# A fused attention and two-layer MoE kernel: batch 0's x transposed in full blocks, batch 1's scores moved into the first softmax, state reads held back

## The chip, the core and the metric

The kernel runs on one core of a Trainium2 chip. The core has TensorE (PE, matmuls and transposes, results into PSUM), ScalarE (ACT, activations and copies), VectorE (DVE, elementwise work and reductions), GpSimd (POOL) and SyncE (SP); SP and POOL issue the loads here. The metric is device time of one execution in microseconds (us), lower is better.

## The reference

```python
# x: (4, 8, 512, 64)   state: (4, 8, 32, 64)
scores = scale * x @ state.T                 # softmax over the 32 state rows
xread  = softmax(scores) @ state             # 512 rows
scores2 = scale * state @ x.T                # softmax over the 512 rows of x
sread  = softmax(scores2) @ x                # 32 rows
attn = concatenate([xread, sread], axis=2)   # (4, 8, 544, 64)
h = tokens(attn) @ w_in                      # 2176 tokens x 512, w_in 512 x 2048
y = (h - tanh(h)) @ w_out                    # w_out 2048 x 512
h2 = y @ w2_in
out = (h2 * tanh(softplus(h2))) @ w2_out
```

The weights are given as float64 and reach the kernel as pairs of 32-bit words. Everything is wanted to float32 precision.

## The kernel before

**Work and order.** The tokens run in the order batch 0, 1, 2, the state rows of all batches ("s"), batch 3; after that the second layer follows in five blocks. A batch of the first layer has 16 steps `t`, one for each 128 columns of `w_in`. A step computes `h` with six matmuls of 512 columns (`up_x`), applies the nonlinearity (`elem1`: one `t` and one `gh` activation on ACT, `t` and `gl` on DVE) and three steps later adds the product with `w_out` into four accumulators (`down_x`, twelve matmuls). Each fp32 product is made of three matmuls of high and low parts (`mm3p`); the first three steps of batch 0 use plain fp32 instead (`PLAIN`), eight longer matmuls a step.

**The fold.** xread is never formed. `sw(b, c)` multiplies the state by `w_in` (tile `swp` in PSUM, `swh` and `swl` in SBUF), once for every four steps, and `up_x` multiplies it by the transposed softmax `AT` (`ath`, `atl`). For batch 0 the first four pieces are made one by one (`sw_first`, `f0` to `f3`).

**Attention of a batch.** Load x (`load_x`, four tiles of 256 KB), transpose it (`xt_t`, PSUM tile `xtp`) and copy it to SBUF (`xt_c`, tile `xt`), scores (`sc_m`, PSUM `sct`), copy (`sc_c`, `scs`), transpose the scores (`sc_t`, `sc`), softmax on DVE and ACT (`sc_max`, `sc_sub`, `sc_exp`, `nm_sum`, `nm_rec`, `nm_mul`: tiles `mx`, `a`, `sm`), transpose the result (`at_a_hi`, `atp`, `ath`). The state read uses the same scores the other way round: `at_exp_t` (softmax along the rows, on `scs`), `at_read_t` (transposes, `e2p`), `at_sread` (matmuls `srd`). State itself is transposed by `state_t` (`stt`, `sbp`, `sbt`).

**Weights.** Each of the 64 weight tiles is a load of 512 KB into one of three buffers (`stage`, tile `st`), and is turned into float32 by `conv_steps`: two activations (`w`, `r`) and a combination on DVE. After the second activation the buffer is free, and the next load goes out on SP's queue. Tiles 1 to 4 are `w_in` of the first 512 columns; after them `w_in` and `w_out` tiles alternate.

**What sets the order.** A scheduler orders the instructions of each engine by the order in which the program emits them and by its own estimates; every engine then works in that fixed order and waits where an operand is missing. The start is written out by hand in `FIRST_STEPS`: up to the bar, PE, ACT and DVE each keep exactly the order of the list (class `Pinned`). The letters: `k` warm-up matmuls on a tile of zeros, `s` state, `x`/`X` transposes of batch 0's x and their copies, `w` the next third of a weight conversion, `c`/`C` scores and copies, `t` `m` `b` `e` `u` `v` `y` the softmax steps, `h`/`l` the halves of `AT`, `f` the pieces of `sw`. After the bar comes the loop over all steps, with side work hung on steps by `at(step, fn)`: for batch 1, loads at steps 1 to 4, transposes at 5 to 8, scores at 9, softmax at 11 to 13, and the state reads of batches 0 and 1 at 19 to 23. Since the scheduler may pull side work forward, parts of it run much earlier than their step. Loads of x go out on SP's queue for batches 0 and 1 and on POOL's for 2 and 3.

**Storage.** 97 SBUF slots of 256 KB are handed out in turn (`get`, `put`). PSUM has eight banks; in the start all but one serve as side banks (`side_bank`), afterwards two (`s0`, `s1`), for `swp`, `xtp`, `sct`, `sc`, `e2p` and `srd`.

Of the kernel before, what the change touches and what calls it, by code (L numbers as in the profile page):

```python
# [29 lines left out]

FIRST_LOADS = "s0123wwwt"
FIRST_STEPS = """
    k4 s0 x0 X0 x1 X1 x2 X2 x3 X3 w0 w0 w0 c0 C0 C1 k2 t0 m0 t1 w1 w1 b0 m1 f0 e0 b1 k12 w2
    u0 v0 y0 e1 w2 h0 u1 v1 y1 h1 l0 w1 l1 | f1 w2 f2 w3 w3 w3 f3
"""
BLOCKS = [4, 4, 4, 3, 2]

# [7 lines left out]
class Pinned:  # L45


    def __init__(self, engine, order):
        self.engine, self.order = engine, order
        self.on, self.last, self.floor = False, None, None  # L50

    def __getattr__(self, name):
        fn = getattr(self.engine, name)

        def call(*args, **kw):
            i = fn(*args, **kw)  # L56
            before = self.last if self.on else self.floor
            if before is not None:
                self.order(i.ins, before)
            if self.on:  # L60
                self.last = i.ins
            return i

        return call
# [3 lines left out]
def attention_moe_kernel(  # L68
# [17 lines left out]
    T = S + NS  # L86
    scale = 1.0 / float(D) ** 0.5

    def order(after, before):
        tc.add_manual_dep(  # L90
            after, before.name,
            mybir.DependencyInfo(mybir.DependencyClass.NoSync, mybir.DependencyReason.DATA),
            reason="activation table",
        )

    TE, AC, V = (Pinned(e, order) for e in (nc.tensor, nc.scalar, nc.vector))
# [13 lines left out]
    def put(*units):  # L110
        for u in units:
            free.append(u.slot)
# [9 lines left out]
    SB = get("sbt")  # L122
    XS = get("xst")
    xst = XS.t.rearrange("p (k n) -> p k n", k=KD)

    def head(b, k, i):
        c = (b * KD + k) * NS
# [109 lines left out]
    X, A, AT = {}, {}, {}  # L237
    XT, SC, ET = {}, {}, {}

    def load_x(b, ks=range(KD)):  # L240
        q = nc.gpsimd if b > 1 else nc.sync
        for k in ks:
            u = get("x", newest=b > 1)
            if b:
                q.dma_start(
                    out=u.t.rearrange("p (r h d) -> p r h d", r=4, h=2),
                    in_=x[b, 2 * k:2 * k + 2].rearrange("h (p r) d -> p r h d", r=4),
                )
            else:
                q.dma_start(  # L250
                    out=u.t.rearrange("p (h c) -> p h c", h=2),
                    in_=x[b, 2 * k:2 * k + 2].rearrange("h (p r) d -> p h (r d)", r=4),
                )
            X[b, k] = u

    def x_tile(b, k, i, r):
        c = r * 128 + i * 64 if b else i * 256 + r * 64
        return X[b, k].t[:, c:c + 64]
# [6 lines left out]
    def xt_t(b, k):  # L265
        P["x", b, k] = ps = side_bank("xtp")
        for r in range(4):
            if b:
                TE.transpose(
                    out=ps[:, r * 128:(r + 1) * 128],  # L270
                    in_=X[b, k].t[:, r * 128:(r + 1) * 128],
                    identity=ident,
                )
                continue
            for i in range(2):
                TE.matmul(
                    out=ps[i * 64:(i + 1) * 64, r * 128:(r + 1) * 128],
                    lhsT=x_tile(b, k, i, r),
                    rhs=ident,
                    start=True,  # L280
                    stop=True,
                )

    def xt_c(b, k):
        XT[b, k] = get("xt")
        AC.activation(out=XT[b, k].t, in_=P.pop(("x", b, k)), func=ACTF.Copy)

    def at_xt(b, k):
        xt_t(b, k)
        xt_c(b, k)  # L290

    def sc_m(b):
        P["c", b, 0], P["c", b, 1] = by_head("sct", b, [[XT[b, k].t for k in range(KD)]])
        put(*(XT.pop((b, k)) for k in range(KD)))

    def sc_c(b, j):
        SC[b, j] = get("scs")
        AC.activation(out=SC[b, j].t, in_=P.pop(("c", b, j)), func=ACTF.Copy)

    def at_scores(b):  # L300
        sc_m(b)
        for j in range(2):
            sc_c(b, j)
# [55 lines left out]
    def at_exp_t(b, j):  # L359
        e = SC.pop((b, j))  # L360
        mt = small.tile([128, 2], F32, tag="mt", name="mt")
        V.tensor_reduce(out=mt[:, 0:1], in_=e.t, axis=AX.X, op=ALU.max)
        V.tensor_scalar(
            out=mt[:, 0:1], in0=mt[:, 0:1], scalar1=-scale, scalar2=None, op0=ALU.mult
        )
        AC.activation(
            out=e.t, in_=e.t, func=ACTF.Exp, scale=scale, bias=mt[:, 0:1], accum_out=mt[:, 1:2]
        )
        V.tensor_scalar(
            out=mt[:, 1:2], in0=mt[:, 1:2], scalar1=1e-9, scalar2=None, op0=ALU.add  # L370
        )
        V.reciprocal(out=mt[:, 1:2], in_=mt[:, 1:2])
        V.tensor_scalar(
            out=e.t, in0=e.t, scalar1=mt[:, 1:2], scalar2=None, op0=ALU.mult
        )
        ET[b, j] = e

    def at_read_t(b, j):
        ps = side_bank("e2p")
        e = ET.pop((b, j))  # L380
        for r in range(4):
            TE.transpose(
                out=ps[:, r * 128:(r + 1) * 128],
                in_=e.t[:, r * 128:(r + 1) * 128],
                identity=ident,
            )
# [127 lines left out]
    def evac(dst, src, i):  # L514
        if i % 2:
            return V.tensor_copy(out=dst, in_=src)
        return AC.activation(out=dst, in_=src, func=ACTF.Copy)
# [216 lines left out]

    side = {}

    def at(step, fn):
        side.setdefault(step, []).append(fn)

    seq = []  # L740
    start = {}
# [16 lines left out]
    for b in (1, 2, 3):  # L758
        for c in range(4):
            at(start[b] + 4 * c - 2, lambda b=b, c=c: sw(b, c))  # L760
    for k in range(KD):
        at(1 + k, lambda k=k: load_x(1, (k,)))
        at(5 + k, lambda k=k: at_xt(1, k))
    at(9, lambda: at_scores(1))
    for j in range(2):
        at(11 + j, lambda j=j: at_exp(1, j))
        at(12 + j, lambda j=j: at_norm(1, j))
        for b in range(2):
            k = 19 + b + 2 * j
            at(k, lambda b=b, j=j: (at_exp_t(b, j), at_read_t(b, j)))  # L770
            if j:
                at(k + 1, lambda b=b: at_sread(b))
    for b in (2, 3):
        at(start[b - 1], lambda b=b: load_x(b))
        for i, f in enumerate(at_steps(b)):
# [28 lines left out]
    def state_t(g, u):  # L804
        ps = side_bank("sbp")
        for e in range(4):
            for i in range(2):
                TE.matmul(
                    out=ps[i * 64:(i + 1) * 64, e * 128:(e + 1) * 128],
                    lhsT=u.t[:, e * 64:(e + 1) * 64],  # L810
                    rhs=ident,
                    start=True,
                    stop=True,
                )
        for i in range(2):
            p = slice(i * 64, (i + 1) * 64)
            AC.activation(
                out=SB.t[p, g * 256:(g + 1) * 256].rearrange("p (e n) -> p e n", n=NS),
                in_=ps[p].rearrange("p (e i n) -> p e i n", i=2, n=NS)[:, :, i, :],
                func=ACTF.Copy,  # L820
            )
        put(u)

    nc.scalar.preload_act_table_set("exp_and_others")
# [22 lines left out]
    def conv_first(f):  # L847
# [3 lines left out]

    steps = {
        "x": lambda k: xt_t(0, k), "X": lambda k: xt_c(0, k), "s": lambda j: state_t(j, st[j]),
        "c": lambda j: sc_m(0), "C": lambda j: sc_c(0, j), "t": lambda j: sc_t(0, j),
        "m": lambda j: sc_max(0, j), "b": lambda j: sc_sub(0, j), "e": lambda j: sc_exp(0, j),
        "u": lambda j: nm_sum(0, j), "v": lambda j: nm_rec(0, j), "y": lambda j: nm_mul(0, j),
        "h": lambda j: at_a_hi(0, j), "l": lambda j: at_a_lo(0, j), "f": sw_first,
        "w": conv_first, "k": keep_warm,
    }
    for e in (TE, AC, V):  # L860
        e.on = True
    for key in FIRST_STEPS.split():
        if key == "|":
            for e in (TE, AC, V):
                e.floor, e.on = e.last, False
        else:
            steps[key[0]](int(key[1:]))
    put(warm)
# [33 lines left out]

    low = 0
    for i in range(len(seq) + 2):
        q = seq[i] if i < len(seq) else None
        prev = [seq[i - k][1:] if start["2"] <= i - k < len(seq) else None for k in range(3)]
        if q:
            up(q)
        if prev[0]:
            up_2(*prev[0], prev[2])  # L910
        elif prev[2]:
            elem2_hi(*prev[2])
        if prev[1]:
# [12 lines left out]
        late_conv(i)  # L926
        AC.on, V.on = pinned
# [33 lines left out]
```

## Time and profile before

| | us |
|---|---|
| median of three runs | 752.68 (751.9 to 754.49) |
| the profiled execution | 752.56 |
| its span, first to last instruction | 750.6 |
| PE busy | 732.5 (98%) |
| DVE busy | 535.1 (71%) |
| ACT busy | 418.1 (56%) |
| POOL busy | 11.0 (1%) |

Times in the rows below are counted from the start of the span. PE's matmuls overlap, so the distance from one start to the next is what a matmul costs, not its own duration. The profiler names every operation recorded through the helper class by line 56, so tiles and operations tell the groups apart.

### The profile page before, as it was taken

What the parts mean: (1) busy time and instruction counts of PE and PEld (TensorE: products, weight loads), DVE (VectorE), ACT (ScalarE), POOL (GpSimd) and SP (SyncE); (2) the same over time, 40 slices, a digit from 0 to 9 for tenths busy, and PEclk for the clock granted to TensorE, in tenths of its full rate; (3) what the DMA queues carried; (4) which work ended last, traced back from release to release, by engine and by line L of the source; (5) the groups of instructions that cost most, each with busy time, mean ns of one, the idle gap of its engine ahead of it and who ended that gap; (6) DMA issues with size and microseconds to landing.
All of it is one profiled execution on the core that took longest, in us unless ns stands there. A gap on an engine that the chain in (4) does not pass through costs nothing.

```text
span 750.6 us, 10527 instructions
## 1 busy us (share of the span) xinstructions
PE 732.5 (98%) x4140; PEld 594.6 (79%) x4140; DVE 535.1 (71%) x985; ACT 418.1 (56%) x779; POOL 11.0 (1%) x14
## 2 busy tenths in 40 slices
PE   8889899999999999999999999999999999999997
PEld 6456687778767898777888888888888888899996
DVE  3767964454538444677698988878887888888896
ACT  5889845344545533688674644444444454545563
POOL 0000020000200000000000000000000000000000
PEclk9999999999999999999999999999999999999999
DMA  9767520000300200253310000100010000100100
GB/s 243 241 208 234 182 57 1 2 1 29 93 20 29 85 29 30 84 169 119 136 56 1 0 1 2 56 1 1 0 57 1 0 1 1 56 1 1 43 1 28
DMA packets 20240, 43.13 MB, mean 57 GB/s; under 512 B 6752, under 2 KB 9824, under 8 KB 20192
## 3 DMA queue, kind: packets, MB, share of 16 engines
q1 hardware_dynamic: 19552, 40.38, 17.0%
q0 software_dynamic: 640, 2.10, 1.0%
q8 instruction: 32, 0.52, 0.3%
q14 instruction: 16, 0.13, 0.1%
HBM read 38.01 MB, written 4.46 MB: 57 GB/s over the span
## 4 chain that ended last, share of the span: by engine, by line
PE 89%; ACT 5%; DMA 3%; DVE 2%; issue 0%; ACTq 0%
PE acc L56 46%; PE h L56 37%; DMA st<-in_moe_w_in_dram 2%; PE swp L56 2%; ACT w L56 1%; PE xtp L56 1%; ACT r L56 1%; PE srd L56 1%; DVE swl L56 1%; ACT swh L56 1%; DMA st<-in_moe_w_out_dram 1%; PE e2p L56 1%; ACT gh L56 1%; PE sc L56 1%; ACT t L56 0%; PE atp L56 0%
## 5 line engine op out<-in xcount | busy, mean ns | idle before, releaser
L56 PE MATMUL h<-yl,wh 128*128 128x512 f32 (+2 forms) x320 | 114.5, 358 | 0.0
L56 PE MATMUL h<-yh,wl 128*128 128x512 f32 (+2 forms) x320 | 114.5, 358 | 0.0
L56 PE MATMUL h<-yh,wh 128*128 128x512 f32 (+2 forms) x320 | 114.4, 357 | 0.0
L56 PE MATMUL acc<-wl,gh 128*128 128x512 f32 x288 | 112.6, 391 | 0.0
L56 PE MATMUL acc<-wh,gh 128*128 128x512 f32 x288 | 112.5, 391 | 0.0
L56 PE MATMUL acc<-wh,gl 128*128 128x512 f32 x288 | 112.5, 391 | 0.0
L56 ACT ACTIVATE er<-er 128x512 f32<-128x512 f32 (+2 forms) x136 | 75.8, 557 | 42.7 <-DVE er L56 40.6
L56 PE MATMUL acc<-gh,wh 128*128 128x512 f32 x244 | 99.2, 407 | 0.0
L56 ACT ACTIVATE er<-h 128x512 f32<-128x512 f32 (+2 forms) x68 | 35.5, 522 | 109.4 <-PE h L56 108.4
L56 DVE TENSOR_TENSOR t<-h,t 128x512 f32<-128x512 f32 x68 | 46.8, 689 | 69.4 <-ACT t L56 69.0
L56 PE MATMUL acc<-gh,wl 128*128 128x512 f32 x244 | 95.6, 392 | 0.0
L56 PE MATMUL acc<-gl,wh 128*128 128x512 f32 x244 | 95.1, 390 | 0.0
L56 DVE SCALAR_TENSOR_TENSOR er<-er 128x512 f32<-128x512 f32 (+2 forms) x136 | 81.3, 598 | 4.7
L56 ACT ACTIVATE t<-h 128x512 f32<-128x512 f32 x68 | 40.4, 594 | 73.2 <-PE h L56 73.0
L56 PEld LDWEIGHTS h<-yl,wh 128*128 128x128 f32 x320 | 60.3, 188 | 8.9 <-DVE yl L56 0.4
L56 PEld LDWEIGHTS h<-yh,wh 128*128 128x128 f32 x320 | 60.3, 189 | 8.8
L56 PEld LDWEIGHTS h<-yh,wl 128*128 128x128 f32 x320 | 60.3, 188 | 7.4
L56 PEld LDWEIGHTS acc<-wh,gl 128*128 128x128 f32 x288 | 54.1, 188 | 11.5
L56 PEld LDWEIGHTS acc<-wh,gh 128*128 128x128 f32 x288 | 54.2, 188 | 11.4 <-ACT t L56 0.8
L56 DVE SCALAR_TENSOR_TENSOR w<-w,r 128x512 uint32<-128x512 uint32 x64 | 43.9, 688 | 26.1 <-ACT r L56 21.6
L56 PEld LDWEIGHTS acc<-wl,gh 128*128 128x128 f32 x288 | 54.1, 188 | 10.2
L56 PEld LDWEIGHTS acc<-gh,wh 128*128 128x128 f32 x244 | 45.9, 188 | 17.2 <-issue 6.5
(95 smaller groups left out, 1198.0 us busy)
## 6 DMA issues: line engine op xcount, KB each, us to landing
st<-in_moe_w_in_dram SPq DMA_DIRECT2D x32, 512.0 KB, 4.1
st<-in_moe_w_out_dram SPq DMA_DIRECT2D x32, 512.0 KB, 4.1
out_dram<-o SPq DMA_DIRECT2D x16, 256.0 KB, 2.2
x<-in_x_dram SPq DMA_DIRECT2D x8, 256.0 KB, 4.8
x<-in_x_dram POOLq DMA_DIRECT2D x8, 256.0 KB, 4.0
stt<-in_state_dram SPq DMA_DIRECT2D x2, 128.0 KB, 4.9
out_dram<-o SPq DMA_DIRECT2D x4, 64.0 KB, 3.5
```

What stands on the lines that cost most here:

```text
L56: i = fn(*args, **kw)
```

## The change

- Batch 0's x is transposed by 16 transposes of 128x128 instead of 32 half-width matmuls (64 instructions). The halves of a transposed block are then two neighbouring rows of x of the same head, not two heads, so the scores (`sc_first`) need the state of each head on both halves of the partitions: `state_t` writes a second copy `sx` for batch 0 with two more activations. Score matmuls are half as wide and twice as many.
- The copies of these transposes and of batch 0's scores alternate between ACT and DVE (`evac`).
- Batch 1's x is loaded on POOL's queue, and only after the last DVE instruction ahead of `L` in the list, the copy `X3`.
- Transposes, copies and scores of batch 1 (`p`, `P`, `q`, `Q`) stand in the hand-written start, in the softmax of batch 0. Two blocks of warm-up matmuls (`k12`, `k2`) become others (`k8`, `k4`, `k2`), and the weight conversions `w` move: the first starts behind the score copies, the third is only begun before the bar.
- State reads of batches 0 and 1 move to steps 20 to 29 and may not be scheduled ahead of the step on which they hang (`back`, `marks`).

```diff
 FIRST_STEPS = """
-    k4 s0 x0 X0 x1 X1 x2 X2 x3 X3 w0 w0 w0 c0 C0 C1 k2 t0 m0 t1 w1 w1 b0 m1 f0 e0 b1 k12 w2
-    u0 v0 y0 e1 w2 h0 u1 v1 y1 h1 l0 w1 l1 | f1 w2 f2 w3 w3 w3 f3
+    k4 s0 x0 X0 x1 X1 x2 X2 x3 X3 L c0 C0 C1 k2 t0 m0 t1 b0 w0 w0 m1 e0 w1 b1 w0 k8 e1 w1 u0 p0
+    P0 p1 P1 f0 v0 y0 p2 P2 u1 v1 h0 p3 P3 y1 k4 h1 l0 w1 l1 w2 q1 Q0 Q1 | f1 w2 w2 f2 w3 w3 w3 f3
 """
...
-    def load_x(b, ks=range(KD)):
-        q = nc.gpsimd if b > 1 else nc.sync
+    def load_x(b, ks=range(KD), after=None):
         for k in ks:
             u = get("x", newest=b > 1)
             if b:
-                q.dma_start(
+                dma = nc.gpsimd.dma_start(
...
+                if after is not None:
+                    order(dma.ins, after, mybir.DependencyClass.Sync)
...
         for r in range(4):
-            if b:
-                TE.transpose(
...
-                continue
-            for i in range(2):
-                TE.matmul(
-                    out=ps[i * 64:(i + 1) * 64, r * 128:(r + 1) * 128],
-                    lhsT=x_tile(b, k, i, r),
-                    rhs=ident,
...
+            TE.transpose(
+                out=ps[:, r * 128:(r + 1) * 128],
+                in_=X[b, k].t[:, r * 128:(r + 1) * 128],
+                identity=ident,
+            )
 
     def xt_c(b, k):
         XT[b, k] = get("xt")
-        AC.activation(out=XT[b, k].t, in_=P.pop(("x", b, k)), func=ACTF.Copy)
+        evac(XT[b, k].t, P.pop(("x", b, k)), 0 if b else k)
...
+    def sc_first():
+        P["c"] = [side_bank("sct") for _ in range(2)]
+        before = None
+        for i in range(2):
+            for k in range(KD):
+                for e in range(2):
...
+                        mm = TE.matmul(
+                            out=P["c"][e][k * NS:(k + 1) * NS, i * 256:(i + 1) * 256],
+                            lhsT=head(0, k, i) if e == i
+                            else SX[e * 64:(e + 1) * 64, k * NS:(k + 1) * NS],
+                            rhs=XT[0, k].t[e * 64:(e + 1) * 64, i * 256:(i + 1) * 256],
...
+    def sc_first_c(i):
+        SC[0, i] = get("scs")
+        for e in range(2):
+            evac(
+                SC[0, i].t.rearrange("p (q e n) -> p q e n", q=2, e=2)[:, :, e, :],
+                P["c"][e][:, i * 256:(i + 1) * 256].rearrange("p (q n) -> p q n", q=2),
+                e,
+            )
...
+    def at(step, fn, back=None):
+        def held():
+            kept = [e.floor for e in engines]
+            for e, m in zip(engines, marks[-back]):
+                e.floor = m
+            fn()
+            for e, m in zip(engines, kept):
+                e.floor = m
+        side.setdefault(step, []).append(held if back else fn)
...
-    for k in range(KD):
-        at(1 + k, lambda k=k: load_x(1, (k,)))
-        at(5 + k, lambda k=k: at_xt(1, k))
-    at(9, lambda: at_scores(1))
...
         for b in range(2):
-            k = 19 + b + 2 * j
-            at(k, lambda b=b, j=j: (at_exp_t(b, j), at_read_t(b, j)))
+            k = start[1] + 4 + 2 * b + 4 * j
+            at(k, lambda b=b, j=j: at_exp_t(b, j), 1)
+            at(k + 2, lambda b=b, j=j: at_read_t(b, j), 1)
             if j:
-                at(k + 1, lambda b=b: at_sread(b))
+                at(k + 3, lambda b=b: at_sread(b), 1)
...
+            if g == 0:
+                AC.activation(
+                    out=SX[p].rearrange("p (k n) -> p k n", n=NS),
+                    in_=ps[p].rearrange("p (e i n) -> p e i n", i=2, n=NS)[:, :KD, 1 - i, :],
+                    func=ACTF.Copy,
+                )
...
+        elif key == "L":
+            load_x(1, after=V.recent)
...
     for i in range(len(seq) + 2):
+        marks.append([e.recent for e in engines])
```

## Rows read from the trace of the kernel before

**Rows 1.** The page, first part: engine, busy us, share of span, instructions.
```profile
PE 732.5 (98%) x4140; PEld 594.6 (79%) x4140; DVE 535.1 (71%) x985; ACT 418.1 (56%) x779; POOL 11.0 (1%) x14
```

**Rows 2.** PE's waits, whole span: us in total, times, longest.
```profile
PE xtp L56 <- DVE swl L56: 3.0, 3, 2.4
PE sc L56 <- DVE swl L56: 2.5, 1, 2.5
...
PE e2p L56 <- DVE swl L56: 1.4, 3, 0.6
PE h L56 <- ACT swh L56: 1.0, 1, 1.0
```

**Rows 3.** Three windows: length, busy us (instructions) of each engine, granted clock, DMA.
```profile
41.21:61.16 19.95, 18.82 (x95) 12.61 (x95) 13.88 (x22) 18.03 (x35) 0.00 (x0) 0.91 0.66 213
61.16:84.57 23.41, 20.69 (x116) 14.76 (x117) 19.82 (x36) 23.05 (x44) 0.00 (x0) 1.00 0.73 226
90.00:100.00 10.00, 10.00 (x104) 8.00 (x103) 9.93 (x24) 6.32 (x12) 1.38 (x1) 1.00 0.10 28
```

**Rows 4.** PE's timeline, 0 to 85: start, duration, operation, count [idle before].
```profile
5.22 4.91 PE L56 MATMUL xtp<-ident,x 128*64 128x128 f32 x64
10.84 1.09 PE L56 MATMUL sct<-xt,sbt 64*32 64x512 f32 x16 [0.70 <-ACT xt L56]
...
20.55 0.48 PE L56 MATMUL h<-ath,swh 128*128 128x512 f32 x1
...
41.21 0.44 PE L56 MATMUL xtp<-ident,x 128*128 128x128 f32 x2 [2.40 <-DVE swl L56]
...
51.29 0.60 PE L56 MATMUL xtp<-ident,x 128*128 128x128 f32 x4
51.65 0.48 PE L56 MATMUL acc<-gh,wh 128*128 128x512 f32 x1
...
61.16 0.50 PE L56 MATMUL h<-ath,swh 128*128 128x512 f32 x1 [1.02 <-ACT swh L56]
...
84.16 0.66 PE L56 MATMUL sc<-ident,scs 128*128 128x128 f32 x4 [2.50 <-DVE swl L56]
```

**Rows 5.** SP's queue, timeline of issues, 0 to 23 us.
```profile
1.25 2.03 SPq L250 DMA_DIRECT2D x<-in_x_dram  x4
...
5.69 8.37 SPq L245 DMA_DIRECT2D x<-in_x_dram  x4
...
17.62 0.34 SPq L166 DMA_DIRECT2D st<-in_moe_w_out_dram  x1
22.59 0.33 SPq L166 DMA_DIRECT2D st<-in_moe_w_in_dram  x1
```

**Rows 6.** ACT's timeline, 0 to 46 us.
```profile
5.49 0.77 ACT L56 ACTIVATE sbt<-sbp 64x256 f32<-64x256 f32 x2 [3.47 <-PE sbp L56]
...
12.03 1.08 ACT L56 ACTIVATE scs<-sct 128x512 f32<-128x512 f32 x2
...
33.95 0.71 ACT L56 ACTIVATE scs<-scs,mt 128x512 f32<-128x512 f32 x1
```

**Rows 7.** DVE's timeline, 0 to 46 us.
```profile
13.38 0.69 DVE L56 TENSOR_REDUCE mx<-sc 128x16 f32<-128x512 f32 x1 [0.71 <-PE sc L56]
...
16.30 0.68 DVE L56 TENSOR_REDUCE sm<-a 128x16 f32<-128x512 f32 x1
...
19.32 0.69 DVE L56 TENSOR_TENSOR a<-a,sm 128x512 f32<-128x512 f32 x1
```

**Rows 8.** Loads of x by issue: queue, count, size, median us to landing.
```profile
x<-in_x_dram SPq DMA_DIRECT2D x1, 256.0 KB, 4.3
...
x<-in_x_dram SPq DMA_DIRECT2D x1, 256.0 KB, 7.9
...
x<-in_x_dram POOLq DMA_DIRECT2D x4, 256.0 KB, 4.0
```

More of the change, by code (lines that the diff above doesn't have):

```diff
@@ L49, in __init__ @@
         self.engine, self.order = engine, order
-        self.on, self.last, self.floor = False, None, None
+        self.on, self.last, self.floor, self.recent = False, None, None, None
     def __getattr__(self, name):
@@ L61, in call @@
                 self.last = i.ins
+            self.recent = i.ins
             return i
@@ L87, in attention_moe_kernel, with order @@
     scale = 1.0 / float(D) ** 0.5
-    def order(after, before):
+    def order(after, before, cls=mybir.DependencyClass.NoSync):
         tc.add_manual_dep(
             after, before.name,
-            mybir.DependencyInfo(mybir.DependencyClass.NoSync, mybir.DependencyReason.DATA),
-            reason="activation table",
+            mybir.DependencyInfo(cls, mybir.DependencyReason.DATA),
+            reason="order of work",
         )
@@ L124, in attention_moe_kernel @@
     xst = XS.t.rearrange("p (k n) -> p k n", k=KD)
+    SX = misc.tile([128, KD * NS], F32, name="sx")
     def head(b, k, i):
@@ L248, in load_x @@
                 )
+                if after is not None:
+                    order(dma.ins, after, mybir.DependencyClass.Sync)
             else:
-                q.dma_start(
+                nc.sync.dma_start(
                     out=u.t.rearrange("p (h c) -> p h c", h=2),
@@ L267, in xt_t @@
         for r in range(4):
-            if b:
-                TE.transpose(
[L270 to L273, printed above, removed]
-                continue
-            for i in range(2):
-                TE.matmul(
-                    out=ps[i * 64:(i + 1) * 64, r * 128:(r + 1) * 128],
-                    lhsT=x_tile(b, k, i, r),
-                    rhs=ident,
-                    start=True,
-                    stop=True,
-                )
+            TE.transpose(
[3 more added lines that the diff above has]
+            )
     def xt_c(b, k):
         XT[b, k] = get("xt")
-        AC.activation(out=XT[b, k].t, in_=P.pop(("x", b, k)), func=ACTF.Copy)
+        evac(XT[b, k].t, P.pop(("x", b, k)), 0 if b else k)
     def at_xt(b, k):
@@ L290, in at_xt @@
         xt_c(b, k)
+    def sc_first():
[4 more added lines that the diff above has]
+                for e in range(2):
+                    with tc.high_priority() if before else nullcontext():
+                        mm = TE.matmul(
[3 more added lines that the diff above has]
+                            rhs=XT[0, k].t[e * 64:(e + 1) * 64, i * 256:(i + 1) * 256],
+                            start=True,
+                            stop=True,
+                        ).ins
+                    if before:
+                        order(mm, before)
+                    before = mm
+        put(*(XT.pop((0, k)) for k in range(KD)))
+    def sc_first_c(i):
[6 more added lines that the diff above has]
+            )
     def sc_m(b):
@@ L735, in attention_moe_kernel @@
     side = {}
-    def at(step, fn):
-        side.setdefault(step, []).append(fn)
+    engines = (TE, AC, V)
+    marks = []
+    def at(step, fn, back=None):
[7 more added lines that the diff above has]
+        side.setdefault(step, []).append(held if back else fn)
     seq = []
@@ L853, in attention_moe_kernel @@
         "x": lambda k: xt_t(0, k), "X": lambda k: xt_c(0, k), "s": lambda j: state_t(j, st[j]),
-        "c": lambda j: sc_m(0), "C": lambda j: sc_c(0, j), "t": lambda j: sc_t(0, j),
+        "c": lambda j: sc_first(), "C": sc_first_c, "t": lambda j: sc_t(0, j),
         "m": lambda j: sc_max(0, j), "b": lambda j: sc_sub(0, j), "e": lambda j: sc_exp(0, j),
@@ L857, in attention_moe_kernel @@
         "h": lambda j: at_a_hi(0, j), "l": lambda j: at_a_lo(0, j), "f": sw_first,
-        "w": conv_first, "k": keep_warm,
+        "w": conv_first, "k": keep_warm, "p": lambda k: xt_t(1, k), "P": lambda k: xt_c(1, k),
+        "q": sc_m, "Q": lambda j: sc_c(1, j),
     }
```

## The prediction

> **What bounds the kernel now.** I read the page first: TensorE (PE) is busy for 98% of the span [rows 1]. Matmul time can only be removed or moved into a hole, so I looked for the holes. The list of PE's waits shows that they are few and early: the largest behind the start are the wait of a batch-1 transpose for a VectorE (DVE) result (longest 2.4), the wait of a `sc` transpose (2.5) and that of an `h` matmul (1.0) [rows 2]. PE's timeline places them before 41.21, 84.16 and 61.16 [rows 4]. Before its first real matmul, `h` at 20.55 [rows 4], PE only prepares: state, x, scores, and warm-up matmuls that fill the softmax. From there on every microsecond of the end is PE work or a PE wait.
>
> The windows say who makes PE wait: ScalarE (ACT) is busy 18.03 of 19.95 us between 41.21 and 61.16, and 23.05 of 23.41 between there and 84.57 [rows 3]. That is the weight conversion, two activations a tile, fed by three load buffers. In the first of these windows the granted clock is 0.91 [rows 3]: the lower of the two levels (1.2 instead of 2.4 GHz) for (1 - 0.91) x 19.95 / 0.5 = 3.6 us, and the window begins where PE had stood idle for 2.40 us. At half rate that cost 1.8 us.
>
> So the end moves by four things: when the first `h` starts, how much PE work lies behind it, what PE waits there, and whether the clock falls.
>
> **The change, part by part.** The sum is made against the profiled execution, 752.56 us (span 750.6); the median of the three runs is 752.68, practically the same.
>
> *A. Batch 1's transposes and scores leave the stream behind the first `h`.* Four 128x128 transposes take 0.36 us, from 51.29 to the next matmul at 51.65 [rows 4]; the four tiles make 1.4 to 1.5. The scores of a batch take 1.1 [rows 4]. In the new order they stand in the softmax gap, where PE runs warm-up matmuls or waits. **-2.6 us**, bounds 0 (if they only lengthen the gap, which B counts) and -2.9.
>
> *B. The first `h`.* Batch 0's x is issued from 1.25 on (four issues in 2.03 us) and lands at most 4.3 us after issue [rows 5, 8], so its last tile is there at about 7.1. Today 64 half-width matmuls take 4.91 us [rows 4]; 16 full transposes need 0.36 us a tile, 0.72 at half clock, and follow the landing. Transposes to 8.2, then the copy, now alternating between ACT and DVE (0.7), give scores at 8.9 instead of 10.84; bounds 8.3 and 10.0. The two extra activations for `sx` (0.39 each at most: the two state copies take 0.77 [rows 6]) end before the last copies are due. Scores 1.1 to 10.0; the score copies, 1.08 for two on ACT [rows 6], are halved over two engines. The first maximum stood 1.35 behind the start of those copies (13.38 - 12.03 [rows 6, 7]); I take 1.15, so 11.2. From the first maximum to the first sum were 2.92 us (16.30 - 13.38 [rows 7]); in the new order a weight combination (0.6) comes in and two small `swl` (0.4) go out: 14.3, the sum ends at 14.9.
>
> Then DVE's order has the `swl` of `f0`, and these hang on batch 1's x: PE runs its program in order, and `p0` and `p1` stand ahead of `f0`. x of batch 1 now waits for the last batch-0 copy (8.9) and goes over GpSimd's (POOL) queue. One issue took 1.38 us on POOL [rows 3], so the second starts at 10.3 and lands 4.0 us later when little else moves [rows 8], 14.4 with some traffic. Transposes 0.4, copy 0.55, the small pieces of `f0` 1.3: DVE goes on at 16.65, so it stands still for 1.75. The rest of the softmax took 3.1 (from the end of the sum, 16.9, to 20.02 [rows 7]): 19.75. From there to the first `h` were 0.53 (20.55 - 20.02 [rows 4, 7]), and the batch-1 scores (`q1`) now stand between: 19.75 + 0.53 + 1.1 = 21.4. Against 20.55 that is **+0.9 us**. Bounds: 19.6 if x lands before DVE needs it (-0.9), and 25.1 if it lands as late as the SyncE (SP) loads did in the crowded start, 7.9 us after issue [rows 8] (+4.5). I take the near end because POOL's own rows are the nearer kind. p2, p3, P2 and P3 hide behind the softmax.
>
> *C. The stall at 41.21 and the low clock.* The wait of 2.40 and the 1.8 of half clock make 4.2 us. The waiting transpose is no longer there. What is late next: `h` of step 4 needs the `sw` pieces of weight tile 11. Weight loads have two sides here. x of batch 1 held SP's queue from 5.69 for 8.37 us [rows 5]; without it loads 4 and 5 go as soon as a buffer is free. But the second activation of the third tile, which frees the buffer for load 6, now stands on ACT behind both copies of `a` and the batch-1 score copies, so load 6 goes at about 23 instead of 17.62, and load 7, behind the fourth tile, at about 25 instead of 22.59 [rows 5]. With three buffers in a ring the lag stays near 2 us up to tile 11. So **-4.2 + 2.0 = -2.2 us**, bounds -4.2 and 0.
>
> *D. The waits at 61.16 and 84.16.* Together 1.02 + 2.50 = 3.5 us [rows 2, 4]; both wait for `sw` pieces that lie in ACT's backlog. From 41 to 84 ACT loses four x copies and two score copies at 0.54 (by the copies in [rows 6]) and one exponential of a state read at 0.71 [rows 6]: 3.9 us less. A backlog of that size would vanish, but a later weight stream (C) eats into it: **-1.8 us**, about half; bounds -3.5 and 0.
>
> *E. State reads of batches 0 and 1 held back* into batch 1. Their PE work stays. ACT and DVE are half idle there, so their work costs nothing while the matmuls cover it; but the reads now share two PSUM banks with batch 2's steps. Reads waited 1.4 us in three places before [rows 2]: **+0.4 us**, bounds 0 and 2. x and scores of both batches hold twelve tile slots longer; I cost that at nothing because late weights are converted only after these reads; without that cover a load of batch 2's x would be late, inside the same 2 us.
>
> Sum: -2.6 + 0.9 - 2.2 - 1.8 + 0.4 = -5.3. 752.56 - 5.3 = **747.3 us**.
>
> **The rivals.** *The x of batch 1 lands late (slower).* PE's order puts p0, p1 ahead of `f0`, p2 ahead of the first transposes of `a`, p3 ahead of the second. Each microsecond that the second tile lands after 12.65 delays the first `h` by one. From 16.1 on (first `h` at 23.1) the 2.6 of A is gone. At the SP loads' 7.9 us the first `h` comes at 25.1, 4.5 later; with 1.8 of low clock after so long a gap, and C and D bringing nothing, 752.56 + 4.5 + 1.8 - 2.6 = 756.3. For it: 256 KB in 256-byte pieces, competing with weight loads. Against: on POOL's queue the same tile took 4.0 us. In the 10 us in which that issue of 1.38 us ran, DVE was busy for 9.93 [rows 3]. The Trainium skill (SBUF — State Buffer, section SBUF: two separate sides) warns that DMAs issued from GpSimd starve of descriptors while DVE runs certain operations that use the shared port; by that rule this rival would be the likeliest, and the 1.38 here does not bear it out. Chance 0.09.
>
> *The clock falls in the softmax gap.* Today one block of warm-up matmuls (`k12`) stands in this gap; the new order has shorter ones and puts waits for x between. If PE idles 2.4 us as at 41.21, the same 3.6 us at half rate follow and cost up to 1.8: 747.3 + 1.8 = 749.1. The Trainium skill (TensorE: Matmul & The Clock Gate, section Part 1: The HAM clock gate) says that the throttled clock is the default and activity releases it; the trace's fall after an idle stretch agrees. Against: transposes and scores lie in the gap as well, and around the wait of 2.50 at 84.16 the clock stayed at 1.00 [rows 3]. Chance 0.13.
>
> *The weights set the pace.* If tile 11 and those after it come 2 to 4 us later and stay so, `h` of steps 4, 8 and 12 waits as today: C and D bring nothing and only A and B are left, 752.56 - 2.6 + 0.9 + 0.4 = 751.3. For it: three buffers and ACT near full. Against: ACT has less to do. Chance 0.18.
>
> *All waits vanish.* -2.6 + 0.9 - 4.2 - 3.5 + 0.2 = -9.2: 743.4. For it: all these waits stand behind work that is taken away. Chance 0.16.
>
> **How the numbers follow.** My forecast (745 to 750) gets 0.44. Its own time is the prediction. About 0.3% (2.3 us) is what a measurement of this kernel can tell from no change; faster means under 750.4. Faster: 0.44 + 0.16, of the clock case 0.12, of the weights case 0.05: 0.77. Slower: most of the first rival, 0.08. Within: the rest, 0.15. Range 742.5 to 751.8: it takes in the last two cases' own times and leaves out the slow rival and the far ends of both sides.
>
> **What would show it.** First batch-0 scores near 8.9, first `h` between 20 and 23 with no `xtp` or `sct` of batch 1 behind it; POOL issues of 1.3 us from 9 us on; load 6 near 23; the wait before step 4 under 2 us and the granted clock 1.0 after it; less PE wait between 55 and 85; state reads between 110 and 140. Wrong it would be through a long wait of `xtp` at 12 to 20, a low clock before 25, or unchanged waits near 40, 60 and 84.

## The result, and the profile after

The changed kernel takes 755.94 us (median of 12 runs, 755.23 to 760.06) against 752.68 (12 runs, 751.6 to 754.9): a ratio of 1.0051, 95% interval 1.0033 to 1.0068 (the ratios here are estimated from all runs and are not the quotient of the two medians). It is slower by half a per cent; 747.3 was forecast, with a range up to 751.8. The profiled execution took 755.38 us, 2.82 more than that of before.

In the fences below, rows of a timeline give start, duration, operation, count and, in brackets, the idle time before it and what ended it. First the page's busy line and granted clock (40 slices) of the changed kernel, then PE's longest waits.

```profile
PE 732.3 (97%) x4108; PEld 593.1 (79%) x4108; DVE 537.0 (71%) x989; ACT 417.6 (55%) x779; POOL 16.2 (2%) x18
...
PEclk9899999999999999999999999999999999999999
```

```profile
PE xtp L56 <- DMA x<-in_x_dram: 3.8, 4, 2.0
PE swp L56 <- DVE w L56: 3.6, 3, 1.4
PE h L56 <- ACT swh L56: 2.3, 2, 1.3
PE sc L56 <- DVE swl L56: 1.7, 1, 1.7
```

Busy sums hardly moved [rows 1]; the waits did. Three of the four lines answer to [rows 2]: the transposes wait above all for x (for `swl` 1.0 is left); `sc` waits less, `h` more, and `swp`, 0.9 in all before, waits 3.6. The page's low clock (8 tenths) now lies in the second slice. PE's timeline of the changed kernel, 8 to 26 us:

```profile
8.16 0.40 PE L56 MATMUL sct<-xt,sbt 64*32 64x256 f32 x1
...
11.47 1.95 PE L56 MATMUL warm<-warm 128*128 128x128 f32 x16
13.88 0.63 PE L56 MATMUL xtp<-ident,x 128*128 128x128 f32 x4 [0.46 <-DMA x<-in_x_dram]
16.47 1.09 PE L56 MATMUL xtp<-ident,x 128*128 128x128 f32 x4 [1.96 <-DMA x<-in_x_dram]
17.49 0.68 PE L56 MATMUL swp<-w,sbt 64*32 64x128 f32 x16
19.11 1.09 PE L56 MATMUL xtp<-ident,x 128*128 128x128 f32 x4 [0.94 <-DMA x<-in_x_dram]
20.32 1.09 PE L56 MATMUL atp<-ident,a 128*128 128x128 f32 x4
21.20 1.06 PE L56 MATMUL xtp<-ident,x 128*128 128x128 f32 x4
22.05 1.47 PE L56 MATMUL warm<-warm 128*128 128x128 f32 x8
23.35 0.60 PE L56 MATMUL atp<-ident,a 128*128 128x128 f32 x4
23.88 1.09 PE L56 MATMUL sct<-xt,sbt 64*32 64x512 f32 x16
24.76 0.42 PE L56 MATMUL swp<-w,sbt 64*32 64x128 f32 x16
25.12 0.50 PE L56 MATMUL h<-ath,swh 128*128 128x512 f32 x1
```

The first `h` starts at 25.12 instead of 20.55 [rows 4]. PE stands for the second tile of batch 1's x until 16.47; only behind it can `f0` (`swp` at 17.49) run. DVE, the same stretch:

```profile
14.49 0.68 DVE L56 TENSOR_REDUCE sm<-a 128x16 f32<-128x512 f32 x1
18.58 0.49 DVE L56 TENSOR_TENSOR swl<-swp,swh 128x128 fp32r<-128x128 f32 x2 [3.42 <-ACT swh L56]
...
21.30 0.69 DVE L56 TENSOR_TENSOR a<-a,sm 128x512 f32<-128x512 f32 x1
```

The sum `sm` comes at 14.49, 1.8 earlier than before [rows 7]; then DVE stands idle for 3.42. Windows of the changed kernel (length, busy us of each engine, granted clock, share of the DMA engines, GB/s) show the clock and the traffic:

```profile
10.00:12.00 2.00, 2.00 (x19) 1.98 (x18) 1.49 (x4) 1.79 (x4) 2.00 (x3) 1.00 1.05 269
14.00:16.00 2.00, 0.51 (x4) 0.27 (x3) 1.17 (x2) 1.67 (x3) 0.55 (x1) 1.00 0.98 292
16.00:18.00 2.00, 1.53 (x20) 0.94 (x20) 0.00 (x0) 0.41 (x1) 0.00 (x0) 0.52 1.12 276
18.00:20.00 2.00, 1.06 (x12) 0.71 (x4) 1.35 (x5) 0.64 (x3) 0.00 (x0) 0.50 0.84 264
20.00:22.00 2.00, 1.88 (x9) 1.72 (x9) 1.89 (x5) 1.16 (x2) 0.00 (x0) 0.50 0.06 20
22.00:24.00 2.00, 2.00 (x22) 1.83 (x28) 1.29 (x2) 0.65 (x3) 0.00 (x0) 0.77 0.00 0
```

After PE was busy for 0.51 of two microseconds, the clock is at its lower level (1.2 GHz) from 16 until nearly 23. The DMA engines are full when x is fetched, 1.05 against 0.10 in the window of POOL's first load in the trace of before [rows 3]. SP's queue of the changed kernel, which answers to [rows 5]:

```profile
11.92 0.37 SPq L167 DMA_DIRECT2D st<-in_moe_w_in_dram  x1
15.21 0.34 SPq L169 DMA_DIRECT2D st<-in_moe_w_in_dram  x1
27.08 0.34 SPq L169 DMA_DIRECT2D st<-in_moe_w_out_dram  x1
28.20 0.33 SPq L169 DMA_DIRECT2D st<-in_moe_w_in_dram  x1
```

Weight loads 4 and 5 go out while x is in flight. Load 6 goes at 27.08 instead of 17.62. The later waits, again PE's timeline of the changed kernel:

```profile
44.09 1.09 PE L56 MATMUL swp<-w,sbt 64*32 64x512 f32 x16 [1.44 <-DVE w L56]
47.54 0.50 PE L56 MATMUL h<-ath,swh 128*128 128x512 f32 x1 [1.30 <-ACT swh L56]
...
65.74 0.50 PE L56 MATMUL h<-ath,swh 128*128 128x512 f32 x1 [0.96 <-ACT swh L56]
80.08 1.09 PE L56 MATMUL swp<-w,sbt 64*32 64x512 f32 x16 [1.32 <-DVE w L56]
85.81 0.66 PE L56 MATMUL sc<-ident,scs 128*128 128x128 f32 x4 [1.69 <-DVE swl L56]
```

Where did the lead change? The n-th `h` matmul starts later than in the trace of before by 4.57 us (first), 6.05 (25th, step 4), 1.62 (97th, at 105 us), 2.81 (193rd, at 190 us), and by 2.8 from there to the end. So three things are to be explained: the start (+4.57), a stretch that gives back only 2.95 of it, and 1.2 us lost between 105 and 190.

### The profile page after: what moved, and what is told of

The parts are those of the page before. It is cut to its first block, busy times and chain, and to the rows that moved or that the text cites. A ratio compares the mean times of both kernels' runs of the same rounds, so it can differ in the third digit from the quotient of the medians.

```text
span 753.6 us, 10473 instructions
## 1 busy us (share of the span) xinstructions
PE 732.3 (97%) x4108; PEld 593.1 (79%) x4108; DVE 537.0 (71%) x989; ACT 417.6 (55%) x779; POOL 16.2 (2%) x18
## 4 chain that ended last, share of the span: by engine, by line
PE 87%; DMA 5%; ACT 4%; DVE 3%; issue 0%; POOL 0%; SPq 0%; ACTq 0%
PE acc L56 45%; PE h L56 36%; DMA st<-in_moe_w_in_dram 3%; DMA x<-in_x_dram 2%; PE swp L56 2%; ACT w L56 1%; ACT r L56 1%; DMA st<-in_moe_w_out_dram 1%; PE srd L56 1%; PE xtp L56 1%; DVE swl L56 1%; PE atp L56 1%; PE e2p L56 1%; ACT gh L56 0%; PE sct L56 0%; ACT t L56 0%
```

## The experiments

The theory: batch 1's x lands late because it shares full DMA engines with weight loads 4 and 5, and PE's fixed order, with `p0` and `p1` ahead of `f0`, makes everything stand behind it. Rivals: POOL's queue itself is slow beside a busy DVE; the half-rate clock alone; the late weight stream; the held-back reads. All ratios are against runs of the kernel before on the same chip; a row stands for ten executions of its kernel, those of before and after for twelve, those of x_pool_now and best1 for four. Profiled executions lie up to 2.6 us from their medians, and the stretch of low clock falls in different places in them; so a trace is read for what happens where, and the verdict is the ratio.

| run | median us | ratio (95%) | first `h` | step 4's `h` | load 6 |
|---|---|---|---|---|---|
| before | 752.68 | | 20.55 | 41.48 | 17.62 |
| after | 755.94 | 1.0051 (1.0033, 1.0068) | 25.12 | 47.54 | 27.08 |
| x_sp | 752.58 | 0.9988 (0.9972, 1.0004) | 23.30 | 45.74 | 25.26 |
| x_sp_wait | 754.25 | 1.0020 (1.0007, 1.0034) | 21.82 | 43.79 | 23.78 |
| x_pool_now | 755.77 | 1.0041 (1.0026, 1.0056) | 24.18 | 46.06 | 26.14 |
| x_pool_alone | 753.83 | 1.0016 (0.9998, 1.0033) | 22.74 | 45.19 | 24.70 |
| f0_early | 756.11 | 1.0039 (1.0022, 1.0056) | 23.82 | 45.05 | 25.80 |
| w2_early | 755.03 | 1.0023 (1.0005, 1.0041) | 25.96 | 45.61 | 16.12 |
| warm_more | 753.48 | 1.0018 (1.0006, 1.0029) | 24.16 | 45.61 | 26.11 |
| no_k4 | 754.51 | 1.0023 (1.0008, 1.0038) | 25.07 | 46.44 | 26.94 |
| full_only | 752.43 | 0.9994 (0.9982, 1.0005) | 20.05 | 42.28 | 17.13 |
| reads_held | 753.23 | 0.9997 (0.9983, 1.0011) | 20.21 | 43.02 | 17.30 |
| reads_free | 754.28 | 1.0018 (1.0007, 1.0028) | 24.36 | 48.20 | 26.31 |
| best1 | 749.67 | 0.9956 (0.9942, 0.9971) | 22.04 | 42.76 | 18.65 |
| best_pool | 752.48 | 0.9990 (0.9973, 1.0006) | 23.31 | 43.62 | 18.50 |
| best_held | 750.53 | 0.9965 (0.9952, 0.9978) | 21.37 | 41.18 | 17.97 |

**Where x comes from.** *x_sp*: the changed kernel, but batch 1's x on SP's queue and without the wait for `X3`.

```diff
-                dma = nc.gpsimd.dma_start(
+                dma = (nc.sync if b == 1 else nc.gpsimd).dma_start(
...
-            load_x(1, after=V.recent)
+            load_x(1)
```

> The changed kernel with one thing undone: batch 1's x goes out on SyncE's queue, without waiting for the last batch-0 copy, as before the change. The instructions of all compute engines keep their order. Theory L (x of batch 1 lands late and blocks TensorE's fixed order): the second x tile is there near 15.5 instead of 16.4 and the last near 17.6 instead of 21.1, the first h starts at 21 to 22.5 instead of 25.1, weight load 6 goes near 24 instead of 27.1, and the time falls by 2.5 to 4 us, to 752 to 753.5. Theory W (the weight stream, held up by the order of ACT's work alone, sets the time): load 6 stays within 1 us of 27, the matmul of step 4 near 47, time 755 to 756.

PE's timeline of x_sp:

```profile
13.99 0.63 PE L56 MATMUL xtp<-ident,x 128*128 128x128 f32 x4 [0.39 <-DMA x<-in_x_dram]
15.12 0.63 PE L56 MATMUL xtp<-ident,x 128*128 128x128 f32 x4 [0.50 <-DMA x<-in_x_dram]
```

The second tile is transposed 1.35 us earlier, DVE stands 1.23 instead of 3.42, and the whole loss is gone (0.9988). In the trace the first `h` (23.30) and load 6 (25.26) come later than expected; the clock is low there from about 18 to 21. *x_sp_wait* keeps the wait and changes the queue alone:

```diff
-                dma = nc.gpsimd.dma_start(
+                dma = (nc.sync if b == 1 else nc.gpsimd).dma_start(
```

> The changed kernel with batch 1's x on SyncE's queue, but still behind the last batch-0 copy. It tells the queue from the wait, both of which the earlier run undid together. If GpSimd's queue is what makes x late, x lands sooner than after the change, the first h comes before 24 and the time is near that run's, 752 to 753.5. If the late issue is (x then shares the DMA engines with weight loads), SyncE's queue needs about 2 us an issue from 9.3 on and holds weight loads 4 and 5 up behind it: x lands no earlier than after the change, 15.5 to 21, the first h stays at 24.5 to 26 and the time at 755 to 757.

x lands 4.9 to 5.6 us after issue although it is issued as late as in the changed kernel (from 8.79); weight load 4 stands behind it on SP's queue and goes at 13.33. First `h` at 21.82, near the 21.4 of the forecast's step B. Its ten runs spread from 752.0 to 755.65; why is open. *x_pool_now* takes the wait alone away:

```diff
-            load_x(1, after=V.recent)
+            load_x(1)
```

> The changed kernel with batch 1's x on GpSimd's queue from the start, without the wait for the last batch-0 copy. If the late issue made x late, x of batch 1 is there before 13, batch 0's x comes 1 to 2 us later for sharing the DMA engines, DVE no longer stands idle before the swl, the first h starts at 21.5 to 23.5 and the time falls to 751.5 to 753.5. If GpSimd's queue itself is slow (its descriptors starve while DVE works), the second x tile still comes after 15 and the time stays above 754.5.

Nothing is won on the whole. Issued on POOL's queue from 1.28 us on, amid the loads of batch 0's x and weights 1 to 3, batch 1's tiles land 6.3 to 10.6 us after issue. They are in time, and no transpose of batch 1 waits for them:

```profile
15.71 1.04 PE L56 MATMUL xtp<-ident,x 128*128 128x128 f32 x8
```

From the scores to the first `h` it now takes 14.17 instead of 16.96. But the early loads delay the others: batch 0's scores start at 10.01 instead of 8.16, and with four executions the ratio is that of the changed kernel within its interval. *x_pool_alone* leaves x on POOL with its wait, but holds weight loads 4 and 5 until the copy `P2`:

```diff
+        if hold[0]:
+            held_loads.append(1)
+            return
...
             load_x(1, after=V.recent)
+            hold[0] = True
...
+            if key == "P2":
+                hold[0] = False
+                for _ in held_loads:
+                    load_next(AC.recent)
```

> The changed kernel with weight loads 4 and 5 held until the copy of batch 1's third x tile; x stays on GpSimd's queue behind the last batch-0 copy, and the compute engines keep their order. If x came late because it shared the DMA engines with these loads, its four tiles land 4 to 5 us after issue, the second before 15, DVE's idle time before the swl falls below 2 us and the first h comes at 22 to 23.5; but the weight stream starts 5 us later, so the time need not fall (752.5 to 756). If GpSimd's queue itself is slow, the second x tile still lands after 16 and the first h stays near 25.

The loads of x by issue in both kernels, those whose issue lies in or reaches into the window from 12 to 13 us (count, size, median us to landing), first the changed kernel, then x_pool_alone:

```profile
x<-in_x_dram POOLq DMA_DIRECT2D x2, 256.0 KB, 7.9
```

```profile
x<-in_x_dram POOLq DMA_DIRECT2D x3, 256.0 KB, 5.3
```

The queue, the wait, the four issues (5.28 us together in both) and the order of DVE's work are the same; only weight loads 4 and 5 go later (18.19 and 18.66). The third and fourth tiles land 5.3 us after issue instead of 7.8 and 7.9. The second, on which `f0` hangs, lands after 5.18 instead of 6.05; PE's timeline of x_pool_alone:

```profile
15.94 0.62 PE L56 MATMUL xtp<-ident,x 128*128 128x128 f32 x4 [1.32 <-DMA x<-in_x_dram]
```

It was expected before 15. No low clock appears before 24, the first `h` comes at 22.74, and the ratio is 1.0016 although the weights start later. So what these loads add is shared DMA engines, not the queue: 2.6 us for the last two tiles, 0.87 for the second. That a second tile takes 5.18 and not 4.0 even so was to be seen in the trace of before, where three loads of x issued 0.9 us apart on POOL's queue (189 to 193 us) landed later than the single ones of [rows 8]:

```profile
x<-in_x_dram POOLq DMA_DIRECT2D x3, 256.0 KB, 4.5
```

The four issues take the same 5.28 us, with DVE busy for 1.97 (after) and 1.93 (x_pool_alone) of the 2 us from 12 to 14, while the landing differs. The Trainium skill (SBUF — State Buffer, section SBUF: two separate sides) says that GpSimd can't write descriptors while DVE runs an operation in a 2-port mode. No run here shows in which mode DVE worked, so none tests that rule.

**The order around it.** Four edits of `FIRST_STEPS` in the changed kernel. f0_early puts `f0` ahead of `p0`; w2_early moves both activations of the third weight tile ahead of the copies of batch 1's x; warm_more adds 18 warm-up matmuls; no_k4 takes the second `k4` out.

```diff
f0_early
-    ... w1 u0 p0
-    P0 p1 P1 f0 v0 y0 p2 ...
+    ... w1 u0 f0 p0
+    P0 p1 P1 v0 y0 p2 ...
w2_early
-    ... k8 e1 w1 u0 p0
-    ... l0 w1 l1 w2 q1 Q0 Q1 | f1 w2 w2 f2 ...
+    ... k8 e1 w1 w2 w2 u0 p0
+    ... l0 w1 l1 q1 Q0 Q1 | f1 w2 f2 ...
warm_more
-    P0 p1 P1 f0 v0 y0 p2 ...
+    P0 k10 p1 P1 f0 k8 v0 y0 p2 ...
no_k4
-    ... P3 y1 k4 h1 ...
+    ... P3 y1 h1 ...
```

> The changed kernel with one step of the hand-written order moved: f0 ahead of p0, so that the small sw pieces, and DVE behind them, no longer wait for x of batch 1. Theory L: DVE's idle time of 3.4 us before the swl at 18.6 goes, but the first transposes of a stay behind p2 (19.1) and the second behind p3 (21.2), so the first h starts at 23 to 24 instead of 25.1 and the time falls by 1 to 2 us. If the block were f0 alone, the first h would come at 21.7 and the time fall by 3.4 us. Theory W: no change beyond 0.7 us.

DVE's idle time falls to 0.40 and the second `a` is divided at 18.02, but `p2` then waits 2.02 at 18.08 with `h0` behind it, and the clock falls later (19.4 to 22.8): the wait moved to the next tile of x. The first `h` comes 1.3 earlier; the ratio is unchanged within its interval.

> The changed kernel with both activations of the third weight tile moved up in ACT's order, to behind those of the second and ahead of the copies of batch 1's x. Load 6 then goes near 16.5 instead of 27.1; the x loads, which share the DMA engines with it, may land up to 1 us later. Theory W: step 4 starts at 41 to 43 instead of 47.5 and the time falls by 3 to 5 us, to 751 to 753. Theory L (only the late first h counts, the weights catch up by themselves): first h 25 to 26, time 755 to 756.5.

Load 6 goes at 16.12, but load 7 at 27.72: one load early in a ring of three. The ratio is 0.28% lower; the two intervals overlap.

> The changed kernel with 18 more warm-up matmuls where TensorE waits for batch 1's x: ten between p0 and p1, eight behind f0. If the half clock between 16 and 23 us is what lengthens the way from the softmax to the first h (warm-up k4, transposes and scores at half rate), the clock stays at full, the first h comes 1.2 to 2 us earlier, 23 to 24, and the time falls by 1 to 2 us. If it is only the late x, the first h stays at 25 or comes later, and the time at 755.5 to 757.

x lands as late after its issue (up to 7.7), yet the clock stays at 1.00 throughout. PE's timeline of warm_more:

```profile
17.37 0.60 PE L56 MATMUL xtp<-ident,x 128*128 128x128 f32 x4
...
24.16 0.50 PE L56 MATMUL h<-ath,swh 128*128 128x512 f32 x1
```

The first `h` comes 0.96 earlier although in this execution batch 0's x landed 1.0 later, and with it the second tile of batch 1. From the transpose of that tile to the first `h` it takes 6.79 instead of 8.65: by these two traces the low clock costs 1.9 of the 4.57 us. The ratio is 0.33% lower.

> The changed kernel without the warm-up block k4 between the two transposes of a. In the trace after the change it lay at half clock from 22.05 to 23.35, while the second half of the softmax was ready at 22.0. If TensorE's fixed order holds these transposes up, the first h comes 1.3 us earlier, near 23.8, and the time falls by about 1 us. If the clock then stays low for longer, nothing is won.

The second `a` transpose starts 1.46 earlier (21.89 instead of 23.35), but PE stays at half rate up to about 24.9, where the scores of batch 1 take 1.71 instead of 0.88, and the first `h` comes at 25.07, no earlier. The ratio is 0.28% lower all the same (overlapping intervals), which the first `h` doesn't explain. It is a poor measure of the median in general: f0_early, with 23.82, is at 1.0039, and x_sp, later there than x_sp_wait and x_pool_alone, has the lowest ratio of the three.

**Full blocks alone.** *full_only*: the kernel before with the 128x128 transposes, `sx`, `sc_first` and the alternating copies, nothing else.

```diff
+            TE.transpose(
+                out=ps[:, r * 128:(r + 1) * 128],
+                in_=X[b, k].t[:, r * 128:(r + 1) * 128],
+                identity=ident,
+            )
...
-        "c": lambda j: sc_m(0), "C": lambda j: sc_c(0, j)
+        "c": lambda j: sc_first(), "C": sc_first_c
```

> The kernel before with only the full 128x128 transposes of batch 0's x (the second copy of the state, half-wide score matmuls, copies on ACT and DVE by turns); orders, loads and state reads as before. Batch 0's scores start near 8.5 instead of 10.84. If the softmax chain carries that through, the first h starts 1.5 to 2 us earlier, near 18.8, and the time falls by 1 to 2 us. If what counts is the weight stream (three buffers, ACT's order), load 6 goes no more than 1 us earlier, the matmul of step 4 stays near 41.5 and the time within 1 us of before.

The scores start at 8.15 instead of 10.84, but the first `h` comes only 0.5 earlier and step 4's 0.8 later: in the order of before the 2.7 us go into other waits.

**The state reads.** *reads_held* is the kernel before with the reads held back; *reads_free* and *best_held* are the changed kernel without, and best1 (below) with that part:

```diff
-            k = 19 + b + 2 * j
-            at(k, lambda b=b, j=j: (at_exp_t(b, j), at_read_t(b, j)))
+            k = start[1] + 4 + 2 * b + 4 * j
+            at(k, lambda b=b, j=j: at_exp_t(b, j), 1)
+            at(k + 2, lambda b=b, j=j: at_read_t(b, j), 1)
```

> The kernel before with the held-back state reads alone. If these cost what the stretch from 105 to 190 us lost after the change, the time rises by 1.2 us, to 754. If the loss there came only from how the scores of batch 2 happened to be split around a state read's transposes, it can be 0. The forecast's part D says that ACT gets 1 us less work before 84 us and the waits near 61 and 84 shrink: down to -1.8 us, 751.

> The changed kernel with the state reads of batches 0 and 1 where they were before, free to be pulled forward. All runs with held-back reads lost 1.2 us between 105 and 190 us, where the score matmuls of batch 2 were split into 2 and 14. Without them the loss should be gone: 1.2 us less, 754.7, if ACT and DVE do not pay it back before 84 us, where the exponentials return; between them the two parts leave 754.3 to 755.6.

> As best1, but the state reads of batches 0 and 1 held back as in the changed kernel. If holding them back costs about 1.2 us between 105 and 190 us by itself (batch 2's score matmuls split in two blocks in PE's order), the time is 1.0 to 2.0 above best1: about 751. If that loss only appears where the weight stream is late, or if the reads' place gives back as much before 84 us (0.4 in the kernel before with held reads), it is 749.7 to 750.3.

All eleven traces with held reads, that of after included, lose 1.13 to 1.19 us against before between 105 and 190 (from the 97th to the 193rd `h`), and none of the four with free reads loses over 0.02. The place, PE's timeline of the changed kernel:

```profile
138.39 1.04 PE L56 MATMUL sct<-xt,sbt 64*32 64x512 f32 x2
139.37 0.50 PE L56 MATMUL acc<-gh,wh 128*128 128x512 f32 x1
...
140.26 1.08 PE L56 MATMUL sct<-xt,sbt 64*32 64x512 f32 x14
141.27 0.50 PE L56 MATMUL acc<-gh,wh 128*128 128x512 f32 x1
```

Batch 2's scores are eight fp32 matmuls of two instructions each. They run in two blocks, one matmul (2 instructions) and seven (14), which take 0.98 and 1.01 from start to next start. In the trace of before they stand in one:

```profile
141.68 1.09 PE L56 MATMUL sct<-xt,sbt 64*32 64x512 f32 x16
142.70 0.50 PE L56 MATMUL h<-atl,swh 128*128 128x512 f32 x1
```

That is 1.02, so the split costs 0.97 of the 1.2. But the total depends on what else holds: on the kernel before, held reads change nothing (0.9997), and best_held is within the interval of best1. Its trace leads that of best1 by 1.87 at 105 us (0.67 of it from the start) and by 0.70 after 190, so the loss is there too; but it is the fastest of its ten executions and best1's the slowest of four, so the traces don't show what makes up for it. In the changed kernel the free reads give back 0.33%. Why held reads gain nothing before 105 there is open.

**Together.** *best1* has x on SP without the wait, free reads, `f0` ahead of `p0`, `p1` behind the first half's division (`y0`), the third weight tile begun early and one more warm-up block `k4`; *best_pool* is the same with x on POOL behind `X3`.

```diff
-    ... u0 p0
-    P0 p1 P1 f0 v0 y0 p2 P2 u1 v1 h0 p3 P3 y1 k4 h1 l0 w1 l1 w2 q1 Q0 Q1 | f1 w2 w2 f2 w3 w3 w3 f3
+    ... u0 f0
+    p0 P0 v0 y0 p1 P1 w2 w2 k4 p2 P2 u1 v1 h0 p3 P3 y1 k4 h1 l0 w1 w2 l1 q1 Q0 Q1 | f1 f2 w3 w3 w3 f3
```

> A candidate that follows theory L: the changed kernel with x of batch 1 on SyncE's queue from the start, f0 ahead of p0, both activations of the third weight tile ahead of the first transposes of a, state reads free as before. Expected: DVE idle under 1 us before the swl, load 6 at 18 to 19, first h at 20.5 to 22 with batch 1's transposes and scores already done, step 4 at 40 to 42, time 748.5 to 751. If the low clock in the gap decides (shorter warm-up blocks), the clock is at half between 16 and 23 again, the first h comes after 23 and the time stays at 752 to 754.

> As best1 (f0's pieces ahead of the transposes of batch 1's x, the third weight tile begun early, state reads free), but batch 1's x on POOL's queue behind the copy X3, as in the changed kernel. If the late landing of x is the cause whatever the order of the other work, tile 3 and 4 land near 19 to 20 us as in the changed kernel, p2 waits for them 2 us, the first h comes between 23 and 24.5 (best1 22.04), and the time is 752 to 754. If the fixed order (p0 and p1 ahead of f0) made the late x matter, the wait is covered by f0 and warm-up matmuls, the first h stays within 1 us of best1 and the time is 750 to 751.

best1 beats both kernels: 749.67 (four executions), ratio 0.9956. Its PE timeline, and two windows:

```profile
17.52 0.60 PE L56 MATMUL xtp<-ident,x 128*128 128x128 f32 x4
17.95 0.60 PE L56 MATMUL atp<-ident,a 128*128 128x128 f32 x4
...
22.04 0.50 PE L56 MATMUL h<-ath,swh 128*128 128x512 f32 x1
```

```profile
16.00:18.00 2.00, 2.00 (x21) 2.00 (x20) 1.76 (x6) 1.92 (x6) 0.00 (x0) 1.00 1.06 271
18.00:20.00 2.00, 2.00 (x21) 2.00 (x20) 1.85 (x5) 2.00 (x5) 0.00 (x0) 1.00 0.97 333
```

No transpose waits for x there, and the clock stays at 1.00. With x on POOL (best_pool) a wait for x of 1.19 at 18.82 is back and the first `h` comes 1.27 later; the ratios differ by 0.34%. So the mended order hides a part of the lateness, not all of it: 0.6% from after to best_pool (order, warm-up and reads), 0.3% from there to best1 (queue and wait). Queue and wait alone gave 0.6% in x_sp, so the effects overlap and don't add.

## Why the prediction was wrong

**A held.** No `xtp` or `sct` of batch 1 lies behind the first `h`; in the trace of before they take 1.58 and 1.02 there, the 2.6 of A. From the first to the 97th `h` the distance is 80.23 us instead of 83.18. The waits shown there grew by 2.24 (9.55 instead of 7.31), and the 1.7 of half rate that the trace of before has near 42 to 45 us is not there; that leaves 2.95 + 2.24 - 1.7 = 3.5 us less work. Of the 0.9 beyond A, 0.3 are the 16 `swp` matmuls of `f1`, which now stand ahead of the first `h`; where the rest went is open.

**B is the step that failed first: its size, by the landing of x.** Up to the first sum it was right: scores at 8.16 (8.9 forecast), sum at 14.49 (14.3), second issue of x at 10.29 (10.3). Then the second tile was taken to land 4.1 us after issue and took 6.05: the transpose starts at 16.47 instead of 14.4. DVE goes on at 18.58 instead of 16.65 (+1.9). The rest of the softmax ends at 21.99, after 3.41 instead of 3.1 (+0.3). From there to the first `h` it takes 3.13 instead of 1.65 (+1.5), because `p3` and the block `k4`, both at half rate, stand ahead of the second `a` transpose, and `f1` ahead of `h`; at full rate, in warm_more, the same stretch takes 1.95. Sum 25.12 instead of 21.4. B's bound of 25.1, for a landing in a crowded start, is met by chance: it put all of the delay on the landing, and half came behind it. The landing was priced by the row nearest in queue, POOL's at 4.0 [rows 8], whose four issues stand 3.5 us and more apart, at a DMA share of 0.10 [rows 3]; the rows nearest in traffic were SP's in the start, up to 7.9. Of the 1.95 that the landing took longer, weight loads 4 and 5 account for 0.87 (x_pool_alone: 5.18), and 1.1 is there without them.

**C came in part.** The wait of 2.40 and the low clock at 41 are gone, as forecast. But load 6 went at 27.08 and not at 23, because ACT's order has its activation behind `h1` and the score copies, all of them later. In the place of the lag of 2.0 stand waits of 1.12, 1.44 and 1.30 before step 4, which starts 6.05 late.

**D went the other way.** The waits between 61 and 87 us are 0.86, 0.96, 1.32 and 1.69, 4.83 in all, against 1.02, 0.22 and 2.50. This isn't the late x alone: best1 starts its first `h` at 22.04 and still waits 1.83 at 42.76, 1.20 at 60.83, 2.11 at 75.99 and 1.61 at 81.65. The waits fit a PE that arrives earlier at the same weight conversions, since work was taken from it; no run isolates that. So without the late start the rival "the weights set the pace" comes nearest: its 751.3 is 1.6 above best1.

**E was too small:** 1.2 instead of 0.4, by the split of batch 2's scores, which no step named.

**The rivals.** "The x of batch 1 lands late" happened, at 0.09: 756.3 was its time, 755.94 came. Its parts are not quite its own: the low clock of 16 to 23 us lies inside the 4.57, not beside it as 1.8 more, C brought something, and E took 1.2. That its time and the measured one agree is in part luck. "The clock falls in the softmax gap" happened too, as a consequence of the late x: warm_more puts it at 1.9 us, near the rival's 1.8, but ahead of the first `h`.

At 105 us the forecast without E was -5.7; +1.62 came. Of these 7.3 us, 3.7 are B. The other 3.6 are in C, D and A; best1, which has no late x, still misses 3.2 of the 7.3 there.

## What to carry to other kernels

Price a load that is moved by rows with the DMA traffic of its new place, not by rows of its queue elsewhere: here loads of the same size on the same queue landed after 4.0, 5.3 and 7.9 us, and loads issued close together landed later than single ones. In a fixed order, count what stands behind each transfer on every engine; work put in a gap fills it only if its operands are there before the gap, otherwise it holds back what the gap was waiting for. Work taken from an engine that meets a stream of other work (here the weight conversion) shortens the time only as far as that stream is ahead, as far as the waits here show.

## What was unexpected of the hardware

- 256 KB loads of x on POOL's queue in the start land 4.2 to 5.3 us after issue with weight loads 4 and 5 held back, up to 7.9 with them (512 KB each), and up to 10.6 amid batch 0's x and weight loads 1 to 3. Four issues take 5.3 to 5.6 us in each case.
- One score matmul alone (2 instructions) costs as much of PE's time as seven (14), 0.98 and 1.01 us, and all eight together 1.02. The order that splits this block pays for it twice, in all eleven traces with held reads.
- Eighteen warm-up matmuls, placed where PE would have stood idle, kept the clock at 1.00 and lowered the ratio by 0.33%, though the x that all waits for came no earlier.
